# Expert 0's weight residuals: from VectorE to ScalarE and GpSimd, with the second search spaced wider

## The chip, the cores and the metric

One Trainium2 chip, one of its cores. The core has a matrix engine (TensorE, PE in the profile), VectorE (DVE), ScalarE (ACT), GpSimd (POOL) and an engine that mostly issues transfers (SyncE, SP). They run at the same time and wait for each other through semaphores. The metric is the device time of one execution in microseconds (us), the median over runs; lower is better.

## The reference, cut to what matters

Attention with two kinds of masks gives 4608 tokens of 512 numbers. A mixture of experts follows: experts and tokens are matched greedily, in order of the logit, until an expert has its 576 tokens; then each expert runs two matrix products with a relu between them.

```python
logits = x @ w_gate                       # x: attention output, [4608, 512]
order = np.argsort(-logits.flatten())
for idx in order:
    tok, e = int(idx) // E, int(idx) % E
    if assigned[tok] >= 0 or counts[e] >= cap:    # cap = 4608 // 8 = 576
        continue
    assigned[tok] = e
    counts[e] += 1
for e in range(E):
    mask = assigned == e
    h = np.maximum(x[mask] @ w1[e], 0.0)          # w1[e]: [512, 1024]
    out[mask] = h @ w2[e]                         # w2[e]: [1024, 512]
```

## The kernel before, in words

The first 205 us are attention and the logits. Then the experts are handled in the order in which they fill up (`ph` 0 to 7). For each of them the kernel finds which expert fills next, and at which logit, by a **search** over thresholds; loads that expert's weights; finds its tokens (`slots`, `indices`); gathers their rows (GpSimd's indirect transfers, tile xr); converts and transposes them (xg, xt); and runs the two layers (`ffn`). Expert 0's search comes alone, ahead of everything. The search for expert 1, its weights and its tokens run beside the matmuls of expert 0, those of expert 2 beside expert 1, and so on.

**Two halves of a weight.** [...] A float32 weight w, scaled by a power of two s, is split into an upper half hi = f16(w*s) and a lower half lo = f16(w*s - hi). `split` (L1011) does this in 8 pieces for w1 (128 columns of the 1024, for all four row blocks: 128 x 512 numbers, interleaved in memory) and 8 for w2 (one row block each, 128 x 512 too): ScalarE writes hi (L1013), VectorE lo (L1014). Before it `square` (L995, ScalarE, tile jk) and `scale` (L1001, a small matmul L1003, L202 to L207) find s. The tokens are split the same way; a product is hi\*hi + hi\*lo + lo\*hi. The float32 weights lie in one buffer for each of w1 and w2, so the next expert's loads wait for the last reader.

**Expert 0's matmuls.** `hidden` makes the first layer in chunks of 128 hidden units. For expert 0 eight chunks are made for rows 0 to 255 first, then eight for rows 256 to 575; each chunk is 12 matmuls, then a relu on ScalarE (hh, L1175) and the lower half on VectorE (hl, L1176). Chunk f needs piece f of w1h and w1l. The chunks' PSUM tiles (ph) cycle through three buffers; the transposes of token tile 2 take one of them between chunk 0 and chunk 1, so chunk 2 takes the buffer of chunk 0. The second layer (L1210, L1216) goes over token tiles 0, 4 (the tail of 64), 1, 2, 3; tile 0 takes the eight pieces of w2h and w2l in turn, 24 matmuls. ScalarE (and for the tail VectorE) takes each result out (y), and GpSimd scatters it to the output (L1227).

**What sets the order.** The kernel emits its instructions along a clock of its own: each matmul adds its nominal cost (109 units for 256 rows, 136 for 320, 123 for 288, 216 and 108 in the second layer), and side chains (`side`: search and slots; `fetch`: indices, gathers, conversions; `spread` and `slowly`: the pieces of weights) are advanced when their due time has passed. What a chain yields is the distance to its next step: in a search round `pace(T_COUNT)`, `pace(T_SUM)`, `pace(T_STEP)`, where `pace` multiplies by PACE1 in expert 1's search alone; T_HOT1 ahead of expert 1's index matmuls (L956), T_HOT for later experts. Each of the R1 = 7 rounds has a comparison on VectorE (cm, L812), nine count matmuls (L828), two small reductions (L831, L834), a folding matmul (L837), a threshold test (L844), a broadcasting matmul (L847) and the next candidates (L850). After the last, the next expert's number (ei) is known and its weights are loaded.

TensorE keeps emission order throughout (`MAN`); inside expert 0's `ffn` ScalarE does too (`MAN0`). The pieces of expert 0's w1 are all emitted ahead of `ffn`; its w2 pieces come from `second` at steps of 1000. VectorE's, GpSimd's and SyncE's orders, and ScalarE's from expert 1 on, are chosen by the compiler's scheduler by priority, before the run. An expert's `ffn` starts being emitted only when its `fetch` has been emitted to its end.

Of the kernel before, what the change touches and what calls it, by code (L numbers as in the profile page):

```python
# [12 lines left out]
AF = mybir.ActivationFunctionType  # L13
OP = mybir.AluOpType
# [33 lines left out]
SHI = CAP // SLO  # L48
URGENT = 4000
T_FIRST, T_COUNT, T_SUM, T_STEP, T_PREFIX, T_NEXT, T_HOT, T_DUP, T_LOAD = 1100, 2950, 1350, 1225, 3900, 2300, 4200, 550, 8000  # L50
PACE1 = 0.55
H0 = 256
HURRY = (0, 1, 7)
MAN, MAN0, MANP = {mybir.EngineType.PE}, {mybir.EngineType.Activation}, (0,)
# [2 lines left out]
T_ROWS, T_ROW = 5000, 1200  # L57
HEAT = (8, 18, 5)
SCALE_AT, TURN_AT, TAKE_AT, SEARCH_AT, TURN_U, W_EARLY, TURNS, TURN_E = 7, 9, 9, 10, 0, 1, 3, 2
T_F, T_LOAD0, T_HOT1, T_W, T_SQ, T_SCALE, T_CUT, T_BULK0 = 3000, 1500, 6350, 4000, 1500, 1500, 1500, 600  # L60
CUT0 = 1
EDGE0, PEAKS, PEAKS_N = 18, (24, 29), (1, 3)
LATE_Q, STORE_Q = (2, 3), (3, 4, 5)
V_BITS, W1_BITS, W2_BITS = 8, 7, 15
# [72 lines left out]
def band_stride_attention_then_capacity_moe(ctx, tc, qt, kl, ks, nl, ns, wg, w1, w2, cst, out, dbg=None):  # L137
    nc = tc.nc
# [593 lines left out]
    def urgent(ph=1):  # L732
        return tc.high_priority(offset=URGENT * (2 if ph == 0 else 1))

    def spread(ph, todo):
        for step, f in todo:
            if ph not in rush:
                yield step if ph else min(step, T_BULK0)
            f()
# [61 lines left out]
    def pace(t):  # L801
        return t if len(closed) > 1 else t * PACE1

# [167 lines left out]
    def weights(ph, ei):  # L971
        e = nc.sync.value_load(ei[0:1, 0:1], min_val=0, max_val=E - 1)
        res, todo = [], []
        for name, w, nch, width, bits in (("w1", w1, DC, FF, W1_BITS), ("w2", w2, FC, DM, W2_BITS)):
            wf = wp.tile([128, nch, width], F32, name=name)
# [6 lines left out]
            k = W_EARLY if ph == 0 and name == "w2" else 4  # L982
# [6 lines left out]
            sc = rt.tile([128, 2], I32, name="w_s" + name)  # L989
            hi = w16.tile([128, nch, width], F16, name=name + "h")  # L990
            lo = w16.tile([128, nch, width], F16, name=name + "l")
# [16 lines left out]
                    return [(slice(0, nch), slice(k, k + 128)) for k in range(0, width, 128)]  # L1008
                return [(slice(k, k + 1), slice(0, width)) for k in range(nch)]

            def split(c, f, k, wf=wf, sc=sc, hi=hi, lo=lo):  # L1011
                s_ = sc.bitcast(F32)[:, 0:1]
                nc.scalar.activation(hi[:, c, f], wf[:, c, f], AF.Copy, scale=s_)  # L1013
                nc.vector.scalar_tensor_tensor(lo[:, c, f], wf[:, c, f], s_, hi[:, c, f], op0=OP.mult,  # L1014
                                               op1=OP.subtract)

            todo.append([(T_SQ, lambda c=c, g=square: g(c)) for c in range(4)])
            todo.append([(T_SCALE, scale)])
# [3 lines left out]
        if ph == 0:  # L1022
# [7 lines left out]
            def more():  # L1030
                with urgent(0):
                    for _, f in cut1[:CUT0]:
                        f()
                g = spread(ph, cut1[CUT0:])
                chains.append([due_now(), g])
# [206 lines left out]
    def due_now():  # L1242
        return clock
# [10 lines left out]
    with tc.manual_schedule(engines=MAN):  # L1254
        work[0] = now[:4] + (now[4](),)
        chains.append([T_LOAD0, load0()])
        for ph in range(E):
            with tc.manual_schedule(engines=MAN0) if ph in MANP else nullcontext():
                while ph not in ready:
                    c = min(chains, key=lambda c: c[0])  # L1260
# [79 lines left out]
```

## Time and profile before

| | |
|---|---|
| median of 3 runs | 696.94 us (696.28 to 700.25) |
| the profiled execution | 691.74 us, its span 690.0 us |
| TensorE busy | 616.1 us, 89% of the span |
| VectorE, ScalarE, GpSimd busy | 460.6, 348.5, 110.5 us |
| expert 0's matmuls | from 238 to 301 us |
| mean granted TensorE clock | 0.939 |

The profile is one execution. Times in its rows are us from the start of the span. A timeline row gives start, duration, engine, line of the kernel, operation, output and inputs, shape, and how many instructions were merged; in brackets stands how long the engine stood idle before it, and what ended that. Busy time of PE is modelled, so the starts of matmuls tell more than their lengths. The granted clock is the share of TensorE's full clock that it was given.

### The profile page before, as it was taken

To read this page: it belongs to the slowest core of one execution; us is meant where nothing else is said; L and a number is where in the kernel's file an instruction comes from. 1 tells how busy PE (TensorE), PEld (TensorE's weight loads), DVE (VectorE), ACT (ScalarE), POOL (GpSimd) and SP (SyncE) were. 2 spreads that over 40 slices of the span, in tenths; PEclk is the share of its full clock that TensorE was granted. 3 is DMA by queue.
4 is the path that set the end of the run, shared out by engine and by line. 5 is a ranking of instruction groups with operands and counts; after the bars stand their busy time and mean duration, and the time that the engine had idled before them with its cause. 6 is when DMAs were issued, how large, how long until landed. Compare 5 with 4: busy or idle time off the path is not lost.

```text
span 690.0 us, 19782 instructions
## 1 busy us (share of the span) xinstructions
PE 616.1 (89%) x8294; PEld 406.7 (59%) x8298; DVE 460.6 (67%) x1389; ACT 348.5 (51%) x567; POOL 110.5 (16%) x124
## 2 busy tenths in 40 slices
PE   6989999899964788989989989999998998999993
PEld 3666777567744365458447537646646745645741
DVE  3757787677857879786787767778768657580200
ACT  2557656575420645681673565384286177771210
POOL 2101110011000300420240150041042041211011
PEclk9579999999975899999999999999999999999997
DMA  8958779777120720860870680491284188821010
GB/s 234 241 157 267 202 212 267 230 228 216 41 67 2 262 75 5 316 132 1 283 168 1 242 188 21 148 255 49 82 290 83 33 295 244 232 51 48 1 39 31
DMA packets 76364, 102.42 MB, mean 148 GB/s; under 512 B 41292, under 2 KB 49062, under 8 KB 75763
## 3 DMA queue, kind: packets, MB, share of 16 engines
q1 hardware_dynamic: 68195, 79.61, 40.4%
q0 software_dynamic: 7360, 21.15, 10.0%
q8 instruction: 65, 1.06, 0.7%
q10 hardware_dynamic: 720, 0.39, 0.2%
q14 instruction: 24, 0.20, 0.1%
HBM read 73.60 MB, written 18.87 MB: 134 GB/s over the span
## 4 chain that ended last, share of the span: by engine, by line
PE 20%; issue 14%; DVE 11%; DMA 10%; ACT 5%; POOL 4%; SPq 1%; POOLq 0%; DVEq 0%; ACTq 0%
PE ph L1168 15%; DMA w<-in_w_dram 6%; DMA xr<-x_scr,idx 3%; POOL xr L1073 2%; PE ph L1216 2%; DVE w1l L1014 2%; ACT jk L995 2%; DVE w2l L1014 2%; POOL out_dram L1227 1%; DVE hl L1176 1%; ACT hh L1175 1%; DMA xt<-xg 1%; DVE xg L1063 1%; DVE cm L812 1%; SPq L980 1%
## 5 line engine op out<-in xcount | busy, mean ns | idle before, releaser
L1168 PE MATMUL ph<-xt,w1h 128*128 128x288 f16 (+2 forms) x1024 | 177.1, 288 | 7.2 <-DMA xt<-xg 5.0
L1168 PEld LDWEIGHTS <-w1h 128*128 128x128 f16 x1024 | 97.3, 98 | 37.9 <-issue 7.7
L1168 PE MATMUL ph<-xt,w1l 128*128 128x288 f16 (+2 forms) x512 | 111.2, 288 | 0.0
L1227 POOL DMA_INDIRECT out_dram<-y,idx x40 | 48.9, 1222 | 332.4 <-ACT y L1226 304.7
L1216 PE MATMUL ph<-w2h,hh 128*128 128x512 f16 x256 | 97.7, 382 | 1.1 <-DVE hl L1176 1.1
L1175 ACT ACTIVATE hh<-ph 128x576 f16<-128x576 f32 (+2 forms) x72 | 42.7, 594 | 110.4 <-PE ph L1168 110.3
L995 ACT ACTIVATE jk<-w 128x1024 f16<-128x1024 f32 x64 | 67.4, 1054 | 60.3 <-DMA w<-in_w_dram 59.2
L1216 PE MATMUL ph<-w2h,hl 128*128 128x512 f16 x256 | 97.7, 382 | 0.0
L1216 PE MATMUL ph<-w2l,hh 128*128 128x512 f16 x256 | 97.5, 381 | 0.0
L1216 PEld LDWEIGHTS <-hh 128*128 128x128 f16 x512 | 49.4, 98 | 58.7 <-issue 8.8
L1176 DVE SCALAR_TENSOR_TENSOR hl<-ph,hh 128x576 f16<-128x576 f32 (+2 forms) x72 | 49.5, 687 | 46.0 <-ACT hh L1175 46.0
L1168 PEld LDWEIGHTS <-w1l 128*128 128x128 f16 x512 | 50.3, 98 | 14.0 <-issue 1.3
L1073 POOL DMA_INDIRECT xr<-x_scr,idx x40 | 41.8, 1046 | 51.7 <-DMA w<-in_w_dram 25.3
L372 ACT ACTIVATE pr<-spa 128x576 f32<-128x576 f32 x32 | 20.8, 651 | 55.9 <-PE spa L369 42.0
L1014 DVE SCALAR_TENSOR_TENSOR w1l<-w,w_sw,w1h 128x512 f16<-128x512 f32 x64 | 45.5, 745 | 4.8 <-ACT w1h L1013 4.8
L1014 DVE SCALAR_TENSOR_TENSOR w2l<-w,w_sw,w2h 128x512 f16<-128x512 f32 x64 | 46.3, 743 | 1.8 <-ACT w2h L1013 1.7
L1216 PEld LDWEIGHTS <-hl 128*128 128x128 f16 x256 | 25.1, 98 | 37.6 <-issue 12.6
L1226 ACT ACTIVATE y<-ph,so 128x512 f32<-128x512 f32 x32 | 21.8, 680 | 45.0 <-PE ph L1216 31.8
L1013 ACT ACTIVATE w1h<-w,w_sw 128x512 f16<-128x512 f32 x64 | 42.4, 708 | 3.0 <-DVE w_sw L207 1.8
L1013 ACT ACTIVATE w2h<-w,w_sw 128x512 f16<-128x512 f32 x64 | 41.2, 710 | 5.4 <-DVE w_sw L207 5.4
L423 POOL DMA_DIRECT2D x_scr<-xs x23 | 14.9, 656 | 170.5 <-DVE xs L407 123.2
L389 PE MATMUL po<-v_s,pr 64*54 64x65 f32 x768 | 33.4, 240 | 4.3 <-issue 4.3
(603 smaller groups left out, 967.1 us busy)
## 6 DMA issues: line engine op xcount, KB each, us to landing
w<-in_w_dram SPq DMA_DIRECT2D x64, 512.0 KB
kl<-in_kl_dram SPq DMA_DIRECT2D x16, 304.0 KB
v_s<-in_ns_dram SPq DMA_DIRECT2D x16, 292.5 KB
v_l<-in_nl_dram SPq DMA_DIRECT2D x16, 292.5 KB
ks<-in_ks_dram SPq DMA_DIRECT2D x16, 288.0 KB
qs<-in_qt_dram SPq DMA_DIRECT2D x16, 288.0 KB
ql<-in_qt_dram SPq DMA_DIRECT2D x16, 288.0 KB
x_scr<-xl SPq DMA_DIRECT2D x8, 512.0 KB
```

The source lines that it names most:

```text
L372: nc.scalar.activation(pr[:, :S].rearrange("k (h n) -> k h n", h=2), u.sp[p][:, :, :HS], AF.Exp, scale=0.125)
L389: nc.tensor.matmul(po[r:r + u.nq, j - j0], pr[k, o:o + u.nq], u.vn[k, t, 2 * p + h], start=(j == j0), stop=(j == j1 - 1), skip_group_check ...
L995: nc.scalar.activation(jk, wf[:, c * n4:(c + 1) * n4].rearrange("p c f -> p (c f)"), AF.Square, scale=1.41422, accum_out=sq[:, c:c + 1])
L1013: nc.scalar.activation(hi[:, c, f], wf[:, c, f], AF.Copy, scale=s_)
L1014: nc.vector.scalar_tensor_tensor(lo[:, c, f], wf[:, c, f], s_, hi[:, c, f], op0=OP.mult, op1=OP.subtract)
L1073: nc.gpsimd.indirect_dma_start(out=xr[:n], out_offset=None, in_=x_rows, in_offset=bass.IndirectOffsetOnAxis(ap=idx[:n, t:t + 1], axis=0))
L1168: nc.tensor.matmul(tile_[:, j, :w], wt[:, d, f * 128:(f + 1) * 128], xt[:, d // 2, xx, d % 2, c], start=(k == 0), stop=(k == 3 * DC - 1))
L1175: nc.scalar.activation(hv, src, AF.Relu)
L1176: nc.vector.scalar_tensor_tensor(lv, src, 0.0, hv, op0=OP.max, op1=OP.subtract)
L1216: nc.tensor.matmul(py, a[:, f, ts_], w[:, f], start=(k == 0), stop=(k == len(todo) - 1))
L1226: nc.scalar.activation(y, py, AF.Copy, scale=so[:, t:t + 1])
L1227: st = nc.gpsimd.indirect_dma_start(out=out_rows, out_offset=bass.IndirectOffsetOnAxis(ap=idx[:n, t:t + 1], axis=0), in_=y[:n], in_offset= ...
```

## The change

Three constants and `split` are edited. W_OWN says how many pieces of expert 0 keep VectorE's subtraction: two of w1, none of w2. For the other 14 ScalarE writes hi as before, then scales the float32 piece in place, and GpSimd subtracts hi from it. All pieces of experts 1 to 7 (`ph` true) stay as they were. PACE1 goes from 0.55 to 0.65, which spaces the steps of expert 1's search wider among expert 0's matmuls, and T_HOT1 from 6350 to 5000, which brings its index matmuls closer behind its slots.

```diff
-PACE1 = 0.55
+PACE1 = 0.65
...
-T_F, T_LOAD0, T_HOT1, T_W, T_SQ, T_SCALE, T_CUT, T_BULK0 = 3000, 1500, 6350, 4000, 1500, 1500, 1500, 600
+T_F, T_LOAD0, T_HOT1, T_W, T_SQ, T_SCALE, T_CUT, T_BULK0 = 3000, 1500, 5000, 4000, 1500, 1500, 1500, 600
 CUT0 = 1
+W_OWN = {"w1": 2, "w2": 0}
...
-            def split(c, f, k, wf=wf, sc=sc, hi=hi, lo=lo):
+            def split(c, f, k, wf=wf, sc=sc, hi=hi, lo=lo, own=W_OWN[name]):
                 s_ = sc.bitcast(F32)[:, 0:1]
                 nc.scalar.activation(hi[:, c, f], wf[:, c, f], AF.Copy, scale=s_)
-                nc.vector.scalar_tensor_tensor(lo[:, c, f], wf[:, c, f], s_, hi[:, c, f], op0=OP.mult,
-                                               op1=OP.subtract)
+                if ph or k < own:
+                    nc.vector.scalar_tensor_tensor(lo[:, c, f], wf[:, c, f], s_, hi[:, c, f], op0=OP.mult,
+                                                   op1=OP.subtract)
+                else:
+                    nc.scalar.activation(wf[:, c, f], wf[:, c, f], AF.Copy, scale=s_)
+                    nc.gpsimd.tensor_tensor(lo[:, c, f], wf[:, c, f], hi[:, c, f], op=OP.subtract)
```

## The prediction

> **What bounds the kernel now.** I read, in this order, the page's engine table, the timeline of each engine between 235 and 305 us, the waits of TensorE, and busy time by stretch.
>
> ```profile
> PE 616.1 (89%) x8294; PEld 406.7 (59%) x8298; DVE 460.6 (67%) x1389; ACT 348.5 (51%) x567; POOL 110.5 (16%) x124
> ...
> 241.30:244.00 2.70, 2.70 (x15) 2.20 (x15) 2.25 (x6) 1.28 (x3) 0.00 (x0) 0.50 0.83 273
> 244.00:256.30 12.30, 9.48 (x105) 8.12 (x104) 9.22 (x28) 4.90 (x11) 0.00 (x0) 0.99 0.22 49
> 256.30:273.50 17.20, 15.42 (x142) 10.69 (x140) 14.99 (x51) 10.82 (x22) 0.00 (x0) 1.00 0.00 1
> 273.50:301.20 27.70, 26.50 (x197) 12.79 (x195) 22.07 (x77) 19.44 (x34) 10.40 (x9) 1.00 0.88 260
> ```
>
> The columns of the four stretches are PE, PEld, DVE, ACT, POOL, then granted clock, DMA share and GB/s. TensorE carries the kernel. Expert 0 is these four stretches: both hidden passes (rows 0 to 255 of the expert, then the other 320), then its second layer. GpSimd is idle in both passes, VectorE is busy 9.2 of 12.3 and 15.0 of 17.2 us. TensorE's losses and the start of the next experts:
>
> ```profile
> 244.66 0.38 PE L1168 MATMUL ph<-xt,w1h 128*128 128x256 f16 x2
> 244.98 0.38 PE L1168 MATMUL ph<-xt,w1h 128*128 128x256 f16 x2
> ...
> 247.24 0.47 PE L828 MATMUL pr__4490<-ohn,cm 128*68 128x32 f16 x9 [1.44 <-DVE cm L812]
> 249.87 0.17 PE L837 MATMUL pr__4490<-r,fold 68*128 68x8 f16 x1 [1.38 <-DVE r L834]
> 252.43 0.45 PE L828 MATMUL pr__4558<-ohn,cm 128*68 128x32 f16 x9
> 256.70 0.43 PE L1168 MATMUL ph<-xt,w1h 128*128 128x320 f16 x2
> 271.47 0.17 PE L847 MATMUL pr__4812<-g,ones_j 128*128 128x8 f16 x1
> 273.53 0.38 PE L1216 MATMUL ph<-w2h,hh 128*128 128x512 f16 x1
> 275.47 0.23 PE L900 MATMUL pr__4929<-sc,tri 128*128 128x72 f16 x2
> 282.84 1.31 PE L956 MATMUL pr__5048<-ohl,rv 128*32 128x64 f16 x36
> 285.71 0.20 PE L964 MATMUL pr__5090<-pick,p 128*64 128x10 f16 x2 [0.81 <-DVE p L959]
> 303.41 0.54 PE L1168 MATMUL ph<-xt,w1h 128*128 128x288 f16 x3 [1.91 <-DMA xt<-xg]
> ...
> 357.96 0.78 PE L1168 MATMUL ph<-xt,w1h 128*128 128x288 f16 x4
> 358.82 0.65 PE L1168 MATMUL ph<-xt,w1h 128*128 128x288 f16 x4
> ```
>
> In the hidden passes TensorE, which runs a fixed order, stands for the search's matmuls behind VectorE (1.44, 1.38). At expert 1 it stands 1.91 us for the transposed tokens (xt), not for weights. At expert 2 four matmuls take 0.78 instead of 0.65: xt arrives just in time there, with no slack. So what moves the end is **when xt of expert 1 and of expert 2 lands**; both chains begin at the index matmuls (L956), whose place among expert 0's matmuls is set by the constants that the change edits.
>
> **The change part by part.** First, the 14 subtractions. Removed from VectorE, put on ScalarE and GpSimd:
>
> ```profile
> L1014 DVE SCALAR_TENSOR_TENSOR w1l<-w,w_sw,w1h x64: 730/746/798, 236.7 to 610.3; 128x512 f16<-128x512 f32 x64
> ...
> 236.74 1.41 DVE L1014 SCALAR_TENSOR_TENSOR w1l<-w,w_sw,w1h 128x512 f16<-128x512 f32 x2
> ...
> 237.82 3.78 ACT L1013 ACTIVATE w1h<-w,w_sw 128x512 f16<-128x512 f32 x6
> 241.95 0.38 ACT L1175 ACTIVATE hh<-ph 128x256 f16<-128x256 f32 x1 [0.35 <-PE ph L1168]
> 265.27 0.44 ACT L1175 ACTIVATE hh<-ph 128x320 f16<-128x320 f32 x1 [1.42 <-PE ph L1168]
> ...
> 247.24 0.42 DVE L1176 SCALAR_TENSOR_TENSOR hl<-ph,hh 128x256 f16<-128x256 f32 x1
> ...
> L246 POOL MEMSET v_s<- 128x1560 f32 x2 | 2.8, 1388 | 0.0
> ```
>
> VectorE loses 14 x 0.75 = 10.4 us. ScalarE gains 14 operations at 3.78 / 6 = 0.63, 8.8 us. A GpSimd subtraction is not in this trace. From below: 0.75, VectorE's price for the shape. From above: the memset writes 1560 numbers in 1.39 us, 0.46 for 512; two reads and a write at that rate are 1.4. I take 1.3, nearer the row of the same engine; both ends stay in the range. [...]
>
> *First pass.* The split of pieces is emitted before the first relu, and ScalarE keeps emission order there (row 237.82 stands before 241.95). Twelve operations now stand where six were: 237.82 + 12 x 0.63 = 245.4. The first relu moves from 241.95 to 245.4, ends at 245.8, its hl (0.42) at 246.2. The third chunk of hidden units takes the PSUM buffer of the first, so it starts at 246.2, not 244.66. Pieces are ready: the last subtraction ends near 246.8 and its chunk comes last. From 246.2 come six chunks of 12 matmuls at 0.11 (the spacing of rows 244.66 and 244.98, three matmuls apart) = 7.9, and two search rounds at about 0.35 each without waits (the count's 0.45 overlaps the next matmul), as VectorE is now free: 254.8, against 256.70. **Gain 1.9.**
>
> *Second pass.* 96 matmuls of 0.109 x 320/256 = 0.136 are 13.1; the wider search leaves three rounds in it (1.1) instead of four; the matmul of w2's scale waits 0.5, because ScalarE is late with its squares; 0.8 for search waits that remain. 254.8 + 15.5 = 270.3, against 273.53. ScalarE needs 1.26 us a piece plus a relu of 0.44 per 1.65 us of matmuls, so its relus lag up to about 2 us; three PSUM buffers hide this (0 as long as the lag is below two chunks, 3.3 us). GpSimd's last piece comes near 272.5, and the second layer needs it 21 matmuls of 0.216 after its start (274.8): hidden, and 2 us of cover. Together **expert 0's second layer starts 3.2 us earlier.**
>
> *Search positions.* A round costs 0.55 x (2950 + 1350 + 1225) + 100 = 3139 units of emission clock (about a ns of matmul), after it 0.65 x 5525 + 100 = 3691. Followed yield by yield (each step comes with the first matmul past its due time), L956 of expert 1 moves from 8.64 to 11.66 thousand units behind the start of the second layer; T_HOT1 has taken 1.35 of it back. The old position agrees with the trace: 282.84 - 273.53 = 9.3 us. New: 270.3 + 11.66 + 0.7 = 282.7. Its operands on VectorE took until 281.9 (row below), 6.4 us behind L900; L900 will be at 277.0, so they may come as late as 283.4. I take 282.9, 0.1 later than before. So the gain of expert 0 is spent on the search's new place.
>
> ```profile
> 280.88 1.02 DVE L948 TENSOR_TENSOR ohl<-sh,iota 128x768 f16<-128x768 f16 x2
> 284.20 0.74 DVE L1224 SCALAR_TENSOR_TENSOR y<-ph,so,yl 64x512 f32<-64x512 f32 x1 [2.29 <-ACT yl L1223]
> ...
> 286.44 0.98 POOL L1073 DMA_INDIRECT xr<-x_scr,idx  x1 [0.30 <-DVE idx L968]
> 292.24 1.40 POOL L1073 DMA_INDIRECT xr<-x_scr,idx  x1 [0.30 <-issue]
> ...
> DMA to landing us min/median/max: 3.4/3.8/5.6
> ...
> 295.87 0.69 ACT L1226 ACTIVATE y<-ph,so 128x512 f32<-128x512 f32 x1 [0.57 <-PE ph L1216]
> 296.98 1.05 ACT L995 ACTIVATE jk<-w 128x1024 f16<-128x1024 f32 x1
> 298.01 0.62 ACT L1062 ACTIVATE xg<-xr 64x512 f16<-64x512 f32 x1
> ```
>
> *What is late next.* L964 waited 0.81 because VectorE first did the tail's y (284.20); that y now comes 3 us earlier, so the gathers start near 285.7, not 286.44. The fifth lands 5.8 + 3.8 later, 295.3. Its conversion stood at 298.01 behind a y that waits for TensorE (295.87) and a square (296.98); that y comes 3 us earlier too, so I put the conversion at 295.8: **expert 1 starts 2.2 us earlier, at 301.2**. TensorE has no work from 270.3 + 26.9 = 297.2 on (27.7 for the layer, less the 0.8 of L964), so it idles 4 us instead of 2.
>
> *The clock.* Long waits cost more than their length:
>
> ```profile
> 575.10 0.28 PE L1168 MATMUL ph<-xt,w1h 128*128 128x288 f16 x1 [0.63 <-DMA xt<-xg]
> 577.89 0.54 PE L1168 MATMUL ph<-xt,w1h 128*128 128x288 f16 x3 [2.52 <-DMA xt<-xg]
> ...
> 578.70:582.00 3.30, 3.30 (x16) 2.05 (x15) 3.03 (x5) 2.04 (x4) 0.00 (x0) 0.50 1.00 353
> 302.00:304.00 2.00, 0.59 (x5) 0.49 (x6) 1.56 (x8) 0.92 (x3) 1.15 (x1) 1.00 0.35 54
> 304.00:306.00 2.00, 2.00 (x21) 1.62 (x20) 1.33 (x2) 1.72 (x3) 0.00 (x0) 1.00 0.34 131
> ```
>
> After a wait of 2.5 us (3.2 with the one before it) the granted clock was 0.50 for 3.3 us, a loss of 1.6; after 1.91 us at expert 1 it stayed at 1.00. Four us lie beyond both: **+1.6**, bounds 0 and 1.7. [...]
>
> *Expert 2.* Its L956 stood 13.8 thousand units ahead of the end of expert 1's matmuls, and will stand 11.9 ahead; from expert 3 on the distance is as before (14.0, 13.8). With no slack (row 357.96) its xt is 1.9 us late; I take **+1.8**; bounds 0 (a faster chain, as at expert 1) and 3.5 (with a halved clock).
>
> *Sum:* -2.2 + 1.6 + 1.8 = +1.2 us. The profiled execution took 691.74 (span 690.0 and 1.74 around it), 0.75% below the median of 696.94 (696.28 to 700.25). Its difference carried over gives 698.1.
>
> **The rivals.** *Taking turns (slower).* VectorE's two-operand instructions on the search's loop (the new candidate, and cm, 0.79) may have to stand aside while GpSimd reads two operands, up to 1.3 each. No row shows GpSimd and VectorE reading together. A round has 3.69 + 0.36 = 4.05 us on TensorE, the free loop takes 3.4 (count at 252.43, next cm done at 255.79, row below), so 0.65 is free, and a round can lose 2 x 1.3 - 0.65 = 1.95.
>
> ```profile
> 254.99 0.80 DVE L812 TENSOR_TENSOR cm<-rmn,cand 128x612 f16<-128x612 f32 x1
> ```
>
> At 1.7 for each of the three rounds beside w2's subtractions expert 0's second layer starts at 275.4, L956 and all behind it 5.1 later: +6.3, **703.2**. It decides from 0.8 us a round on. For it: TensorE's order leaves no way round. Against: between two subtractions GpSimd waits for ScalarE. [...]
>
> *The gain is kept (faster).* The conversions of expert 1 follow their gathers without any hold: 285.7 + 5.8 + 3.8 + 0.62 + about 3.7 from conversion to first matmul (as 298.01 + 0.62 to 303.41 is 4.8, less 1.1 of queueing) = 299.6, -3.8; the wait is then 2.4 us, the clock stays, and expert 2's chain closes up as well, to 0. **693.1.** For it: ScalarE's holds of before. Against: the token conversions of expert 1 are emitted later, the last four behind the y of 295.87.
>
> *The subtractions don't leave ScalarE free.* If writing a piece in place had to wait until GpSimd has read the piece before (they interleave in memory), a piece would cost 0.63 + 1.3, the first relu would come near 250, all 4.6 later: **702.7**. Against: ScalarE wrote piece 3 at 237.82 while VectorE still read piece 2 of the same tile (236.74 + 1.41 = 238.15).
>
> **How the numbers follow.** Forecast 0.50, own range 694.5 to 700.4; taking turns 0.21; in-place wait 0.04; gain kept 0.25. From 0.5% on (3.5 us) a measurement of this kernel can tell a difference. Nearly all of the forecast lies within it; the slow rivals are slower, the fast one faster by a little more than that: faster 0.24, same 0.50, slower 0.26. The range takes the fast rival (692.5) and the slow ones (703.5) in.
>
> **What would show it.** Right: the first relu of expert 0 on ScalarE near 245.4, expert 0's second layer from about 270, L956 within 1 us of 282.84, expert 1 from about 301 after a wait of 3 to 5 us with clock 0.50 behind it, a new wait for xt at expert 2. Wrong: search matmuls waiting over 0.8 us each in the second pass, subtractions far from 1.3 us, expert 2 starting without a wait, or experts 3 to 7 shifting against each other.

## The result, and the profile after

The changed kernel took 704.6 us (median of 19 executions) beside 696.94 us for the kernel before (19 executions); the ratio is 1.0129, 95% interval 1.0097 to 1.0161. (Ratios and intervals leave out the executions that were slowed as a whole, medians don't, so a ratio is not the quotient of the two medians.) It is **slower by 1.3%**, some 8 to 9 us. The forecast was 698.1 with a range from 692.5 to 703.5, so it missed. The profiled execution took 701.34 us (span 699.6), the one before 691.74 (span 690.0).

To read where the 9.6 us between the two profiles arise, three matmuls of the kernel before are needed: the first of expert 0, the first of expert 1's second layer, and the first of expert 3.

```profile
237.97 0.27 PE L1168 MATMUL ph<-xt,w1h 128*128 128x256 f16 x1 [1.03 <-ACT xt L1055]
...
328.28 0.38 PE L1216 MATMUL ph<-w2h,hh 128*128 128x512 f16 x1
...
413.99 0.65 PE L1168 MATMUL ph<-xt,w1h 128*128 128x288 f16 x4
```

The same places and the waits of TensorE in the changed kernel, from its timeline (lines lie 1 to 5 further down: L1173 is the first layer, L1221 the second, L957 the index matmuls, L965 what follows them, L1004 the matmul of a weight's scale):

```profile
238.91 0.27 PE L1173 MATMUL ph<-xt,w1h 128*128 128x256 f16 x1 [0.74 <-ACT xt L1060]
...
243.34 0.27 PE L1173 MATMUL ph<-xt,w1l 128*128 128x256 f16 x1
247.92 0.38 PE L1173 MATMUL ph<-xt,w1h 128*128 128x256 f16 x2 [4.31 <-ACT xt L1060]
...
273.10 0.39 PE L1221 MATMUL ph<-w2h,hh 128*128 128x512 f16 x1
...
280.57 0.24 PE L901 MATMUL pr__4973<-sc,tri 128*128 128x72 f16 x2
...
286.36 1.29 PE L957 MATMUL pr__5060<-ohl,rv 128*32 128x64 f16 x36
...
288.33 0.20 PE L965 MATMUL pr__5102<-pick,p 128*64 128x10 f16 x2
...
304.68 0.16 PE L1004 MATMUL pr__5299<-ss,ones_b 128*128 128x1 bf16 x1 [2.31 <-DVE ss L1002]
304.78 0.28 PE L1173 MATMUL ph<-xt,w1h 128*128 128x288 f16 x1
307.50 0.42 PE L1173 MATMUL ph<-xt,w1h 128*128 128x288 f16 x1 [2.44 <-DMA xt<-xg]
...
335.15 0.38 PE L1221 MATMUL ph<-w2h,hh 128*128 128x512 f16 x1
...
366.59 0.54 PE L1173 MATMUL ph<-xt,w1h 128*128 128x288 f16 x3 [0.36 <-DMA xt<-xg]
...
422.70 0.65 PE L1173 MATMUL ph<-xt,w1h 128*128 128x288 f16 x4
```

The busy time of its engines over the whole span, from the page:

```profile
PE 617.5 (88%) x8294; PEld 405.3 (58%) x8298; DVE 453.6 (65%) x1375; ACT 357.4 (51%) x581; POOL 127.3 (18%) x138
```

And its busy time by stretch (PE, PEld, DVE, ACT, POOL; then granted clock, DMA share, GB/s):

```profile
247.92:252.00 4.08, 4.08 (x29) 3.19 (x30) 3.03 (x5) 1.57 (x4) 4.08 (x5) 0.58 0.26 51
252.00:273.10 21.10, 20.77 (x198) 15.85 (x196) 15.49 (x54) 17.10 (x33) 10.01 (x8) 1.00 0.06 10
273.10:304.78 31.68, 27.70 (x205) 13.17 (x205) 22.79 (x79) 21.18 (x38) 15.51 (x13) 1.00 0.78 231
307.50:313.00 5.50, 5.50 (x25) 3.52 (x26) 3.55 (x11) 2.56 (x4) 0.00 (x0) 0.50 0.01 3
```

The work moved as it should: VectorE has 7 us less, ScalarE 9 and GpSimd 17 us more. TensorE's own work is the same (8294 matmuls); it lost time waiting and at half clock. From expert 0's first matmul to expert 3's first ("the stretch" from here on), 176.02 us became 183.79, and this holds 7.8 of the 9.6 us:

| part of the stretch | before | after | difference | forecast |
|---|---|---|---|---|
| first matmul to expert 1's tokens (303.41; 307.50) | 65.44 | 68.59 | +3.15 | -2.2 |
| on to expert 1's second layer (328.28; 335.15) | 24.87 | 27.65 | +2.78 | +1.6 |
| on to expert 3's first matmul (413.99; 422.70) | 85.71 | 87.55 | +1.84 | +1.8 |

The other 1.8 us lie ahead of expert 0 (0.94) and behind expert 3's first matmul (0.89), where nothing was edited. Single executions differ by more than that: expert 0's first matmul comes between 234.4 and 245.0 us in the traces of this case.

**How much of it is clock.** Summed in steps of 0.5 us, the time that the granted clock took from the stretch (1 minus the clock, times the step) is 3.4 us before and 5.1 after. The kernel before has half clock there too: once beside expert 0's first two chunks, once in expert 2's second layer. So between these two traces 1.7 of the 7.8 us are clock and some 6 are waits. Over the executions behind the ratios, each with its mean granted clock, an estimate is that time x clock grew by 3.9 us (656.8 to 660.7) and time x (1 - clock) by 4.1 (39.3 to 43.4), each give or take 2: on average about half of the loss is clock.

**The first layer of expert 0** took 34.19 us instead of 35.56. Its gain is small because TensorE stood 4.31 us ahead of the third chunk, then ran 4.08 us at 0.58 of its clock. ScalarE's timeline, and a row of VectorE's, show what it stood for:

```profile
238.74 0.72 ACT L1014 ACTIVATE w1h<-w,w_sw 128x512 f16<-128x512 f32 x1
239.50 0.72 ACT L1019 ACTIVATE w<-w,w_sw 128x512 f32<-128x512 f32 x1
240.12 0.71 ACT L1014 ACTIVATE w1h<-w,w_sw 128x512 f16<-128x512 f32 x1
...
246.95 0.36 ACT L1180 ACTIVATE hh<-ph 128x256 f16<-128x256 f32 x1
247.22 0.59 ACT L1060 ACTIVATE xt<-ph 128x512 f16<-128x512 f32 x1
...
247.35 0.42 DVE L1181 SCALAR_TENSOR_TENSOR hl<-ph,hh 128x256 f16<-128x256 f32 x1 [2.69 <-ACT hh L1180]
```

Twelve operations take 8.21 us (0.68 each), and only then comes the first relu, 8.04 us after the first matmul instead of 3.98. The third chunk's buffer waits for the relu and its lower half. The profile names the copy xt behind the relu, which ends at 247.81; the lower half ends at 247.77, 0.15 us ahead of the chunk at 247.92. In a later run (e13) the lower half ends at 249.42 and the chunk again comes 0.15 behind it, at 249.57, though xt had ended at 249.27; so it is most likely the lower half. All of them stand behind the twelve operations.

**Behind expert 0's second layer** the index matmuls come 13.26 us after the layer's start (9.31 before), and expert 1's matmuls run on, with the last of its tokens, 4.1 us later than before on the trace's clock. TensorE is out of work by then: it waits 2.31 us for the scale of expert 1's w2 and 2.44 for the tokens, and then runs 5.5 us at half clock.

### The profile page after: what moved, and what is told of

It reads as the page before. It is cut to its first block, busy times and chain, and to the rows that moved or that the text cites. A ratio compares the mean times of both kernels' runs of the same rounds, so it can differ in the third digit from the quotient of the medians.

```text
span 699.6 us, 19801 instructions
## 1 busy us (share of the span) xinstructions
PE 617.5 (88%) x8294; PEld 405.3 (58%) x8298; DVE 453.6 (65%) x1375; ACT 357.4 (51%) x581; POOL 127.3 (18%) x138
## 4 chain that ended last, share of the span: by engine, by line
PE 48%; issue 15%; DVE 13%; DMA 10%; ACT 8%; POOL 4%; SPq 1%; POOLq 0%; ACTq 0%; DVEq 0%
PE ph L1173 17%; PE po L390 6%; PE ph L1221 5%; PE spa L347 4%; DMA w<-in_w_dram 3%; DMA xr<-x_scr,idx 3%; DMA xt<-xg 3%; POOL xr L1078 2%; PE spb L441 2%; PE spb L502 2%; PE spa L370 1%; DVE w1l L1016 1%; ACT w L1019 1%; PE spb L461 1%; POOL out_dram L1232 1%
## 5 line engine op out<-in xcount | busy, mean ns | idle before, releaser
L1173 PE MATMUL ph<-xt,w1h 128*128 128x288 f16 (+2 forms) x1024 | 178.9, 291 | 12.5 <-DMA xt<-xg 5.6
L1173 PEld LDWEIGHTS <-w1h 128*128 128x128 f16 x1024 | 98.5, 99 | 43.4 <-DMA xt<-xg 6.2
L1173 PE MATMUL ph<-xt,w1l 128*128 128x288 f16 (+2 forms) x512 | 112.4, 291 | 0.0
L1221 PE MATMUL ph<-w2h,hh 128*128 128x512 f16 x256 | 97.1, 379 | 0.3 <-DVE hl L1181 0.3
L1221 PE MATMUL ph<-w2h,hl 128*128 128x512 f16 x256 | 97.0, 379 | 0.0
L1221 PE MATMUL ph<-w2l,hh 128*128 128x512 f16 x256 | 97.0, 379 | 0.0
L1221 PEld LDWEIGHTS <-hh 128*128 128x128 f16 x512 | 48.6, 98 | 63.2 <-issue 12.8
L1173 PEld LDWEIGHTS <-w1l 128*128 128x128 f16 x512 | 50.5, 99 | 14.5 <-issue 1.5
L1078 POOL DMA_INDIRECT xr<-x_scr,idx x40 | 41.3, 1031 | 56.8 <-DVE L L922 25.2
L1221 PEld LDWEIGHTS <-hl 128*128 128x128 f16 x256 | 25.0, 97 | 34.7 <-issue 9.2
L1016 DVE SCALAR_TENSOR_TENSOR w1l<-w,w_sw,w1h 128x512 f16<-128x512 f32 x58 | 41.0, 743 | 5.0 <-ACT w1h L1014 5.0
L1016 DVE SCALAR_TENSOR_TENSOR w2l<-w,w_sw,w2h 128x512 f16<-128x512 f32 x56 | 40.5, 742 | 1.6 <-ACT w2h L1014 1.4
L1068 DVE TENSOR_TENSOR xg<-xr,xg 128x512 f16<-128x512 f32 (+1 forms) x37 | 25.9, 705 | 17.3 <-ACT xg L1067 17.2
```

The source lines that it names most:

```text
L1068: nc.vector.tensor_tensor(xs[:, 1], xv, xs[:, 0], op=OP.subtract)
L1078: nc.gpsimd.indirect_dma_start(out=xr[:n], out_offset=None, in_=x_rows, in_offset=bass.IndirectOffsetOnAxis(ap=idx[:n, t:t + 1], axis=0))
L1173: nc.tensor.matmul(tile_[:, j, :w], wt[:, d, f * 128:(f + 1) * 128], xt[:, d // 2, xx, d % 2, c], start=(k == 0), stop=(k == 3 * DC - 1))
L1221: nc.tensor.matmul(py, a[:, f, ts_], w[:, f], start=(k == 0), stop=(k == len(todo) - 1))
```

## The experiments

The theory after the result: **two losses**. (1) Six doubled pieces of w1 hold the first relu on ScalarE; TensorE idles and is slowed. (2) The wider spacing takes the search's waits out of expert 0's first layer, but places the index chains of experts 1 and 2 so late that the time is lost again, with a half clock on top. Rivals: the GpSimd subtractions themselves cost (late start, or VectorE standing aside); the late squares of w2 cost; the lost time is expert 2's.

All runs are against the kernel before on the same chip. "Run on" is when expert 1's matmuls run on after the last wait for tokens; all us are counted from expert 0's first matmul and come from one execution each, the ratio from many.

| run | pieces on GpSimd | constants | first relu | first layer | run on | stretch | ratio (95%) |
|---|---|---|---|---|---|---|---|
| before | 0 | old | 3.98 | 35.56 | 65.44 | 176.0 | 1 |
| e1 | 14 | old | 8.04 | 35.86 | 65.75 | 176.8 | 0.9995 (0.9958 to 1.0033) |
| e4 | w2's 8 | old | 4.55 | 36.03 | 66.44 | 176.8 | 1.0004 (0.9964 to 1.0044) |
| e2 | 0 | new | 3.52 | 30.92 | 64.20 | 179.5 | 1.0068 (1.0031 to 1.0106) |
| e5 | w2's 8 | new | 4.16 | 31.65 | 65.24 | 181.1 | 1.0045 (1.0007 to 1.0084) |
| e9 | 3 + 8 | new | 5.79 | 32.66 | 66.57 | 180.0 | 1.0123 (1.0053 to 1.0193) |
| **after** | 14 | new | 8.04 | 34.19 | 68.59 | 183.8 | 1.0129 (1.0097 to 1.0161) |
| e8 | 14 | PACE1 old | 8.04 | 36.24 | 66.78 | 177.8 | 1.0030 (0.9989 to 1.0070) |
| e11 | 14 | new, places back | 8.05 | 34.20 | 65.89 | 177.6 | 1.0038 (0.9993 to 1.0083) |
| e7 | 0 | new, places back | 3.51 | 30.79 | 62.91 | 174.9 | 0.9982 (0.9945 to 1.0020) |

### The two halves of the change alone

e1_split_only: the 14 subtractions with the old constants.

```diff
-PACE1 = 0.65
+PACE1 = 0.55
...
-... T_HOT1, ... = 3000, 1500, 5000
+... T_HOT1, ... = 3000, 1500, 6350
```

> The 14 subtractions on GpSimd, the old constants (PACE1 0.55, T_HOT1 6350). Theory A (the loss comes from the search's new place: TensorE reaches expert 1's index matmuls 3 thousand units later, and the chains of experts 1 and 2 with them): expert 0's first layer starts its second part about as in the changed kernel (34 to 35 us after its start), the wait at expert 1 is that of before or less, and the time is the kernel before's, -2 to +2 us. Theory B (the loss comes from the split: ScalarE's in-place scaling holds the first relu, TensorE idles 4.3 us and its clock is halved behind it): +5 to +9 us.

e2_const_only: the constants with every subtraction on VectorE.

```diff
-W_OWN = {"w1": 2, "w2": 0}
+W_OWN = {"w1": 8, "w2": 8}
```

> The new constants alone (PACE1 0.65, T_HOT1 5000), all 16 subtractions on VectorE. Theory A: slower by 4 to 9 us: a wait of 2 us or more for w2's scale and another for xt at expert 1, clock 0.50 behind it, and 1 to 3 us at expert 2. Theory B: -2 to +2 us, since the first layer is as before and its search waits are shorter.

e4_w2_only: the old constants, and only w2's eight pieces on GpSimd.

```diff
+PACE1 = 0.55 and T_HOT1 = 6350, as in e1
-W_OWN = {"w1": 2, "w2": 0}
+W_OWN = {"w1": 8, "w2": 0}
```

> Only the eight pieces of w2 on GpSimd, all of w1 on VectorE, old constants. The first relu is not held, so there is no idle time of 4 us in the first pass and no halved clock behind it. Theory A: 0 to 3 us faster than the kernel before, as three rounds of the search no longer share VectorE with w2. Theory B: the same as A here, but 5 us or more faster than the kernel with all 14 pieces and the old constants; under A the difference between the two is under 3 us.

Measured: 697.37, 702.04 and 695.99 us beside 698.66. The subtractions alone change nothing that could be told, all of them or w2's; the constants alone cost 0.7%; both together cost 1.3%, where the sum of the two is 0.6, give or take 0.5. In e1 the relu is held just as long (8.04 us), and TensorE waits as well:

```profile
251.19 0.59 PE L1173 MATMUL ph<-xt,w1h 128*128 128x256 f16 x2 [2.49 <-ACT xt L1060]
```

But from this third chunk on (9.01 us after the first matmul, 6.69 before) the layer needs 26.85 us instead of 28.87, since VectorE answers the search sooner: no search matmul waits over 0.3 us there. The hold and this gain cancel. In e2 the first layer is the shortest of these, 4.6 us under before, and the second layer with the wait at its end takes 4.8 us more than the 27.7 before; busy time in the two layers, and behind it the wait at the end of the second, from the timeline:

```profile
239.49:270.41 30.92, 27.24 (x263) 21.05 (x263) 27.88 (x84) 20.11 (x40) 0.00 (x0) 1.00 0.21 63
270.41:302.94 32.53, 27.73 (x206) 13.08 (x204) 23.47 (x80) 19.35 (x34) 11.63 (x10) 1.00 0.79 230
```

```profile
302.84 0.16 PE L1004 MATMUL pr__5285<-ss,ones_b 128*128 128x1 bf16 x1 [3.23 <-DVE ss L1002]
```

So each half alone takes away the same thing, TensorE's waits for VectorE in the search (1.44 and 1.38 before; 0.57 and 0.82 in e2, none in e1). Behind the third chunk the changed kernel takes 25.18 us, e1 26.85: where the spacing has taken most of the waits away, the subtractions have little left to win, and their hold is nearly a plain loss.

### The held relu

e5_new_w2 puts w1's six pieces back on VectorE; e9_three_pieces puts three of them back. Both keep the new constants.

```diff
-W_OWN = {"w1": 2, "w2": 0}
+W_OWN = {"w1": 8, "w2": 0}     # e5
+W_OWN = {"w1": 5, "w2": 0}     # e9
```

> The changed kernel with the six w1 pieces back on VectorE: only the eight w2 pieces are subtracted by GpSimd, with both new constants. The stretch from expert 0's first matmul to expert 3's first (short: the stretch to expert 3) took 176.0 us before, 179.5 with the constants alone and 183.8 in the changed kernel. Theory A (the w1 pieces hold the first relu on ScalarE, TensorE stands 4.3 us for it and runs at half clock afterwards; w2's pieces cost nothing, as with the old constants): expert 0's first layer falls from 34.2 to about 31 us, the stretch to about 179.5, the time to that of the constants alone, 0.6 to 0.8% above before. Rival B (any subtraction on GpSimd costs once the search is spaced wider, for instance through VectorE's loop): first layer over 33, time 1.0 to 1.3% above before.

> The changed kernel with three of w1's six pieces back on VectorE (pieces 5 to 7 and all of w2 stay on GpSimd), both new constants. Theory A (what costs is that ScalarE does two operations a piece ahead of the first relu, at 0.74 us the second): the first relu comes 3 x 0.74 = 2.2 us earlier against expert 0's first matmul, TensorE's wait before the third chunk falls from 4.3 to 1.5 to 2.6 us, expert 0's first layer from 34.2 to 32 to 33.3, time 0.5 to 1.0% above before (between the 0.45% with no w1 piece and the 1.29% with six). Rival B (not the number of pieces, but that GpSimd is used in the first pass at all): wait over 3.5 us, first layer over 33.8, time as the changed kernel.

e5 came out at 1.0045 (0.6 to 0.8% was expected), its first layer at 31.65 us, so w1's six pieces cost the changed kernel about 0.8%, give or take 0.5. Its stretch of 181.1 is over the 179.5 expected. In e9 the first relu comes 5.79 us after the first matmul, 2.25 us sooner, and the wait is 2.38:

```profile
248.11 0.36 ACT L1180 ACTIVATE hh<-ph 128x256 f16<-128x256 f32 x1
...
249.07 0.38 PE L1173 MATMUL ph<-xt,w1h 128*128 128x256 f16 x2 [2.38 <-ACT xt L1060]
```

Relu, wait and layer (32.66) follow the number of doubled pieces as expected. The ratio, 1.0123, is above the expected 1.005 to 1.010, with an interval too wide (1.0053 to 1.0193) to tell half of the loss from all of it.

### GpSimd's late first subtraction

In the changed kernel GpSimd did nothing for 8.46 us ahead of its first subtraction, although the first scaled piece was there at 240.2. The instructions of that line, with durations as min/median/max in ns, and the timeline:

```profile
L1020 POOL TENSOR_TENSOR w1l<-w,w1h x6: 1143/1146/1602, 246.8 to 253.3; 128x512 f16<-128x512 f32 x6
L1020 POOLq MODIFY_POOL_CONFIG  x2: 42/42/43, 238.3 to 238.4; - x2
```

```profile
246.81 7.62 POOL L1020 TENSOR_TENSOR w1l<-w,w1h 128x512 f16<-128x512 f32 x6 [8.46 <-ACT w1h L1014]
```

Two configuration instructions of 0.04 us stand at its start. The trace has no busy time of GpSimd's in the 8.46 us, 6.6 of them behind the first scaled piece, and what fills them is not shown. e3_early_gpsimd and e10_early_clean put a tiny subtraction behind the all-reduce at 206 us, to see whether the gap then falls earlier.

```diff
     nc.gpsimd.partition_all_reduce(rng, pk, 128, bass.bass_isa.ReduceOp.max)
+    early = r1.tile([128, 1], F32, name="early")
+    nc.gpsimd.tensor_tensor(early, rng, pk, op=OP.subtract)    # e3
+    nc.gpsimd.tensor_tensor(early, pk, pk, op=OP.subtract)     # e10
```

> The changed kernel, with one more GpSimd subtraction of a single column right after its reduction over partitions at 206 us, so that its first subtraction of weights is not the first of its kind. In the changed kernel GpSimd stood idle for 8.46 us between 238.35 and 246.81 although the first scaled piece lay ready at 240.2. If that was a change of GpSimd's program, the first subtraction now starts at 240 to 241. Theory C (the late subtractions hold TensorE in the first pass): 3 to 5 us faster than the changed kernel. Theories A and B: no faster than it by more than 1 us, for TensorE's third chunk (247.92) waits for the first relu and its hl (end 247.77) as well.

> The changed kernel with one tiny two-operand GpSimd operation put behind the all-reduce, this time on data that nobody waits to write again, so that GpSimd's 8.5 us before its first subtraction fall where it has nothing to do. Theory A (the late start of GpSimd does not set the pace, ScalarE's two operations a piece do): subtractions from within 2.5 us of the first scaled piece, TensorE's wait before the third chunk still 4.0 to 4.6 us, first layer 34 to 35, time within 0.4% of the changed kernel. Rival B (the late subtractions hold the chunks of the first pass): wait under 3 us, first layer under 33, time 0.4% or more below the changed kernel.

e3 took 714.06 us (1.0242, 1.0194 to 1.0289), but it measured another thing: its tiny operation reads rng, which VectorE then overwrites, and VectorE stood 7 us for that gap, just ahead of the first search.

```profile
212.32 0.15 DVE L709 TENSOR_SCALAR rng<-rng 128x1 int32<-128x1 int32 x1 [6.99 <-POOL early L708]
```

e10 avoids that. GpSimd's first subtraction now starts at once, and the relu comes exactly when it did, 8.05 us after the first matmul at 243.88:

```profile
245.27 1.16 POOL L1022 TENSOR_TENSOR w1l<-w,w1h 128x512 f16<-128x512 f32 x1 [3.85 <-ACT w L1021]
...
251.93 0.36 ACT L1182 ACTIVATE hh<-ph 128x256 f16<-128x256 f32 x1
```

The ratio is 1.0147 (1.0082 to 1.0212), no better than the changed kernel: ScalarE's order sets the pace, not GpSimd. The wait ahead of the third chunk was 2.72 and the layer 32.95, both outside the theory's numbers and inside the rival's. The third chunk started 9.03 us after the first matmul, as in the changed kernel (9.01); the first two chunks took 6.31 us of that (9.03 less 2.72) beside 4.70 there, and the rest of the layer 23.92 beside 25.18. By these times an estimate is that in this execution the half clock fell on the first two chunks, which filled part of the wait, and not behind it.

### The late squares of w2

e6_squares_early brings expert 1's weight preparation forward, so that the scale of w2 is no longer late.

```diff
+        if ph == 1:
+            todo = [(min(s, T_W if i == 0 else 1000), f) for i, (s, f) in enumerate(todo)]
```

> The changed kernel with one edit: for expert 1 the steps of its weight preparation stand 1000 units apart instead of 1500, so that the last squares of w2 are emitted before the end of expert 0's matmuls and not behind them. Theory A (the 2.31 us wait for the scale of w2 covers the wait for the transposed tokens that follows it; the tokens land no sooner): the wait for the scale falls under 0.5 us, the wait for the tokens grows from 2.4 to 4 to 5 us, expert 1's hidden matmuls run on from within 0.7 us of where they did, time within 0.3% of the changed kernel. Rival B (the late squares are the cost): expert 1 about 2.3 us earlier, time 0.3 to 0.6% below the changed kernel.

The wait for the scale of w2 is gone, and the wait for tokens is twice as long; the half clock stays (timeline of TensorE, then the stretch behind it with its clock of 0.52).

```profile
311.25 0.28 PE L1175 MATMUL ph<-xt,w1h 128*128 128x288 f16 x1 [2.50 <-DMA xt<-xg]
314.05 0.42 PE L1175 MATMUL ph<-xt,w1h 128*128 128x288 f16 x1 [2.52 <-DMA xt<-xg]
```

```profile
314.05:319.50 5.45, 5.45 (x26) 3.50 (x27) 3.91 (x9) 2.00 (x4) 0.00 (x0) 0.52 0.01 3
```

Expert 1 runs on after 69.08 us, 0.5 later than in the changed kernel; the ratio is 1.0116 (1.0069 to 1.0163), not told apart from it. The edit moved the squares of expert 1's w1 as well, and its token indices came 0.6 us later against expert 0's first matmul, so the test is not clean. But expert 1 followed its tokens, and the 2.31 us of the changed kernel only covered a wait for them.

### The place of the index chains

e8_pace_back undoes PACE1 alone in the changed kernel. e7_places_back keeps the new constants with all subtractions on VectorE and sets three places back; e11_changed_places does this in the changed kernel.

```diff
-PACE1 = 0.65
+PACE1 = 0.55                                   # e8
...
-        yield T_PREFIX
+        yield 2000 if ph == 1 else T_PREFIX    # e7, e11: with e6's edit, and
-... (T_F if 1 < ph < E - 1 else 0) ...
+... (1000 if ph == 2 else T_F if 1 < ph < E - 1 else 0) ...
```

> The changed kernel with one constant undone: the search's spacing 0.55 again, T_HOT1 stays 5000, all 14 pieces on GpSimd. Theory A (the wider spacing is what moves the index chains of experts 1 and 2 and what leaves TensorE without work while the first relu is held): stretch to expert 3 of 175 to 177.5 us, as with the split alone (176.8), time within 0.4% of before. Rival B (the index matmuls brought nearer to the prefix matmul by T_HOT1 now wait for VectorE, and are the loss): a wait of 0.5 us or more at the index matmuls of expert 1, time 0.5% or more above before.

> The constants alone (all pieces on VectorE), with expert 1's weight steps 1000 units apart, the prefix matmul of expert 1 due 2000 instead of 3900 units after its number, and expert 2's index chain due 1000 instead of 3000 units after its prefix matmul. Theory A (the wider spacing shortens expert 0's first layer by 4 to 5 us; all of it is lost again because the index chains of experts 1 and 2 and expert 1's squares are late against the matmuls): the stretch to expert 3 falls from 179.5 to 173 to 176 us, the time to 0 to 0.6% below before. Rival B (the loss of the constants is not in these places, but in waits that follow from elsewhere, such as the gathers or ScalarE's load): stretch 178 to 180, time still 0.5% or more above before.

> The changed kernel, 14 pieces on GpSimd, with the three places set back (expert 1's weight steps 1000 units apart, its prefix matmul due 2000 instead of 3900 units after its number, expert 2's index chain due after 1000 instead of 3000). Theory A (two separate losses: the late index chains and the held relu): the places give back what they gave back to the constants alone, about 0.9%, the held relu stays: first layer 34 to 35, stretch to expert 3 from 183.8 to 177 to 180, time 0.2 to 0.7% above before. Rival B (they are one loss: with the relu held the places do not matter, or the other way round): time over 1.0% above before, or first layer under 32.

With the old spacing (e8) the loss falls from 1.29% to 0.30%, which can't be told from none; the stretch of 177.8 is just over the 177.5 expected. The rival's wait is there too, as T_HOT1 = 5000 brings the index matmuls ahead of what they read, but it does not decide:

```profile
284.68 1.50 PE L957 MATMUL pr__5031<-ohl,rv 128*32 128x64 f16 x36 [1.07 <-DVE rv L943]
```

With the places back, the constants alone go from 1.0068 to 0.9982 and the whole change from 1.0129 to 1.0038: 0.9% both times (give or take 0.5), as the theory has it. In e11 the first layer stays at 34.20 (the held relu), and expert 1 runs on 2.7 us sooner than in the changed kernel, at full clock:

```profile
307.10:313.00 5.90, 3.85 (x32) 2.96 (x33) 5.44 (x17) 4.89 (x9) 1.09 (x1) 1.00 0.40 95
```

In the stretch the two losses are separate and nearly add up: against the changed kernel, places back (e11) takes off 6.2 us, w1 back on VectorE (e5) 2.7, and both (e16, below) 8.3. In the whole time only the loss of the places is clear; e16 doesn't come out below e11. e7 (696.15 us beside 697.71) beats the changed kernel, but cannot be told from the kernel before.

### Which place, and a better version

e12_places_rows is e7 with the token conversions of expert 1 due 800 instead of 1200 units apart. e13_expert1_back and e14_expert2_back set back expert 1's and expert 2's places one at a time in the changed kernel; e15_constants_expert1 sets back expert 1's with the constants alone; e16_w2_places is e11 with w1 on VectorE.

```diff
-            yield T_ROWS if t == 0 else T_ROW
+            yield T_ROWS if t == 0 else 800 if ph == 1 else T_ROW    # e12
```

> The constants alone with the three places set back, as the run that came out at 0.9982, and with the token conversions of expert 1 due 800 instead of 1200 units apart, so that the last two are emitted ahead of a square. Theory A (expert 1's first matmuls still wait 0.75 and 2.25 us for tokens whose conversion stands behind other work on ScalarE): that wait falls by 1 to 1.5 us, time 0.3 to 0.6% below before. Rival B (the transposing transfers and the weight loads set the landing): wait unchanged within 0.5 us, time 0 to 0.3% below before.

> The changed kernel with expert 1's places set back alone (its weight steps 1000 units apart, its prefix matmul due after 2000 instead of 3900 units). All three places together took 1.0129 to 1.0038 of before. Theory A (expert 1's chain is most of the loss, expert 2's about 1.8 us as predicted): expert 1's hidden matmuls run on within 66.5 us of expert 0's first matmul (68.6 in the changed kernel) with no half clock behind, expert 2 still waits; ratio to before 1.004 to 1.008. Rival B (expert 2's chain is most of it): ratio 1.009 or more.

> The changed kernel with expert 2's index chain alone set back (due after 1000 instead of 3000 units). Theory A: expert 1 as in the changed kernel (hidden matmuls run on 68 to 69 us after expert 0's first, clock 0.50 behind), the time from there to expert 3's first matmul 1 to 2.5 us shorter than the changed kernel's 115.2; ratio to before 1.009 to 1.012. Rival B: ratio 1.007 or less.

> The constants alone, with expert 1's places set back and expert 2's left late. If setting expert 2's chain back is what lengthens the stretch behind expert 3 (267 to 269 us in the three runs that had it, 264 to 266.7 in nearly all others), this run has 264 to 266.5 there, a stretch to expert 3 of 175.5 to 177.5, and a ratio to before of 0.997 to 1.001. If that is scatter between executions, the stretch behind may come out anywhere from 264 to 269, and the ratio is 0.999 to 1.004.

> The changed kernel with w1 on VectorE, only w2's eight pieces on GpSimd, and all three places set back. Theory A (both losses of the change taken away, w2's pieces cost nothing): first layer of expert 0 under 31.8 us, stretch to expert 3 of 174 to 177, ratio to before 0.996 to 1.001. Rival B (w2's pieces cost something once the places are back): stretch over 177.5, ratio over 1.002.

| run | first layer | run on | stretch | behind the stretch | ratio (95%) |
|---|---|---|---|---|---|
| e12 | 30.78 | 62.79 | 175.9 | 267.3 | 1.0035 (0.9990 to 1.0079) |
| e13 | 34.95 | 66.58 | 182.5 | 266.0 | 1.0084 (1.0046 to 1.0121) |
| e14 | 34.98 | 69.84 | 186.3 | 268.8 | 1.0129 (1.0056 to 1.0202) |
| e15 | 30.79 | 62.56 | 176.3 | 269.4 | 1.0025 (0.9987 to 1.0063) |
| e16 | 30.00 | 61.91 | 175.5 | 271.9 | 1.0055 (1.0022 to 1.0088) |

Expert 1's places alone give back 0.45% (e13), and 0.43% with the constants alone (e15), each give or take 0.5: in e13 expert 1 runs on 2.0 us sooner than in the changed kernel, after 66.58, but the clock behind that is 0.69 for 5.5 us, where the theory had no loss. Expert 2's place alone (e14) gives nothing, against the expectation; with expert 1's the two give 0.9% (e11), but the intervals are too wide to say that expert 2's has a share. In e12 the wait for the tokens of expert 1 fell as expected, from 2.25 to 1.10 us, and the time did not: 1.0035, over both theories' numbers, though not told apart from e7's 0.9982. e16 has both losses taken away, shows it in the first layer and the stretch, and is still 0.55% slower than before, a miss. (A cost of w2's pieces does not explain this: e12 and e15, which have none on GpSimd, show the same behind the stretch.)

What e16 loses against the kernel before, and e12 and e15 within their intervals, lies behind the stretch, which itself is as short as before (175.5 to 176.3; 176.0 before): from expert 3's first matmul to the last they take 267.3 to 271.9 us, where the kernel before took 264.3 and the changed one 265.2. e7 and e11 have it too (268.8 and 269.1), and e7 has the lowest ratio of all, so this is not a fixed price. e15 has it without expert 2's edit, so that edit alone is not the cause. The traces show where it arises. The granted clock costs 3.4 to 5.1 us there in these five runs, 1.7 before and in the changed kernel. In e15 and e16 TensorE also waits longer for VectorE in the second layers of experts 3 and 4, mostly for the sums of the searches that run there: 8.6 and 7.5 us in all, 4.6 before. Over all executions e16's time x clock is 657.1 us beside the 656.8 of the kernel before, its time x (1 - clock) 42.0 beside 39.3: by this estimate most of what it loses is clock. **Why the clock and these waits get worse there stays open.**

## Why the prediction was wrong, point by point

**Right in direction.** The held relu, the index chain that spends the gain of the first layer, a halved clock behind expert 1's wait, and 1.8 us up to expert 3 were all forecast; so was a GpSimd subtraction of 1.3 us (1.15 measured). **The step that failed is the term for expert 1's start:** it was put 2.2 us earlier than before and came 3.2 later, counted from expert 0's first matmul. Four sizes in it were too kind (the first layer by 1.9 us, the distance to the index matmuls by 0.7, the step to the gathers by 0.9, the gathers to the tokens by 1.95), the clock term behind it was too small by 1.2, and all errors go the same way.

**The first layer: a gain of 3.2 forecast, 1.4 measured.** The third chunk was put 8.2 us after the first matmul; it came after 9.0, since a doubled piece takes ScalarE 1.37 us and not 1.26. The rest was put at 24.1 us and took 25.2: the prediction had TensorE wait for the chunk (the search no longer filled the time), but charged no clock for it. The stretch behind it ran at 0.58, which costs 4.08 x 0.42 = 1.7 us; without that the 24.1 would have been 0.6 too long. At expert 1 the prediction had put a half clock behind a long wait, from the 0.50 for 3.3 us that the trace of the kernel before shows behind 2.52 us.

**L956: forecast 282.9, measured at 286.36 (now L957).** 2.8 us of that is the later start of the second layer (273.10, not 270.3; 0.9 of it from ahead of expert 0), 0.7 the distance.

**From the index matmuls to the gathers: 2.8 forecast, 3.69 measured, 3.60 before.** L965 lost its wait, as predicted, but another took its place. VectorE's indices stood behind the sum of expert 1's w1 squares, which waits for ScalarE:

```profile
289.55 0.16 DVE L1002 TENSOR_REDUCE ss<-sq 128x1 bf16<-128x4 f32 x1 [1.61 <-ACT jk L996]
289.62 0.16 DVE L968 CAST idx<-pr__5102 128x10 int32<-128x10 f32 x1
...
290.05 0.99 POOL L1078 DMA_INDIRECT xr<-x_scr,idx  x1 [2.82 <-DVE idx L969]
```

**From the first gather to expert 1: 15.5 forecast, 17.45 measured, 16.97 before.** The prediction let ScalarE's holds of the last conversion go; the chain did not get shorter. These three steps and the first layer make expert 1's start a loss of 3.2 us, where 2.2 were to be gained.

**The clock at expert 1: +1.6 forecast, +2.8 measured.** TensorE had not waited 4 us but 2.31 and 2.44 with two short matmuls between, and the half clock behind that lasted 5.5 us and not 3.3.

**Expert 2: +1.8 forecast, +1.84 measured**, but hardly for the reason given. The new wait for its tokens was 0.36 us. In expert 2's second layer TensorE waited 4.5 us in all, mostly for VectorE's share of the next search, where it had waited 2.1 before; but before, that layer had lost 1.7 us to the clock, and now none. The longest such waits, before and after:

```profile
404.61 0.17 PE L837 MATMUL pr__6690<-r,fold 68*128 68x8 f16 x1 [2.13 <-DVE r L834]
...
413.91 0.17 PE L838 MATMUL pr__6703<-r,fold 68*128 68x8 f16 x1 [2.55 <-DVE r L835]
```

And e14, with expert 2's chain set back, was no faster. That the figure came out is luck: it is the rest of other terms, and the mechanism is not shown.

**Taking turns** got a chance of 0.21 and was not the cause, though the time came out near its number. VectorE's instructions do get longer beside GpSimd's subtractions: the token residual took 1.20 instead of 0.69, one candidate step 0.65 instead of 0.24, and one step that adds a column to a table (pre, L821) 1.2 instead of 0.23 (the row holds two instructions). A comparison that started just ahead of a subtraction, at 267.17, kept its 0.80, and there the subtraction took 1.77 instead of 1.15 (the first of the three in GpSimd's row).

```profile
251.10 1.20 DVE L1068 TENSOR_TENSOR xg<-xr,xg 64x512 f16<-64x512 f32 x1
...
253.82 0.65 DVE L851 SCALAR_TENSOR_TENSOR cand<-steps,pr__4511,pre 128x18 f32<-128x18 f32 x1 [0.32 <-PE pr__4511 L848]
264.07 1.35 DVE L821 TENSOR_SCALAR pre<-steps,cand 128x18 f32<-128x18 f32 x2
267.17 0.80 DVE L813 TENSOR_TENSOR cm<-rmn,cand 128x612 f16<-128x612 f32 x1
...
267.20 4.16 POOL L1020 TENSOR_TENSOR w2l<-w,w2h 128x512 f16<-128x512 f32 x3 [0.58 <-POOL w2l L1020]
```

No search matmul of TensorE waited over 0.3 us in the second pass, and e4 prices w2's subtractions at nothing that could be told (1.0004, 0.9964 to 1.0044). Where the two ran together the trace has 0.4 to 1.0 us more in VectorE's instruction (1.20, 0.65 and 1.2 us) or 0.6 more in GpSimd's (1.77); which of the two pays is not shown. **Gain kept** fell with the gather chain, and the **in-place wait** did not show: ScalarE went on from piece to piece, 1.37 us apart, while GpSimd had not begun.

## What to carry to other kernels

Two edits that take away the same wait can't add their gains, while their costs both stay: run each alone before they are priced together. A step put on an engine that keeps an order is paid by whatever stands behind it there (here the first relu, 8.04 us after the first matmul instead of 3.98). And TensorE paid again in its clock behind some of its waits (1.7 us behind the 4.31 in the changed kernel, nothing behind the 1.91 at expert 1 in the kernel before), so such a wait needs a second price, with bounds.

## What the runs showed of the hardware

In the traces of the kernel before and of the changed one the half clock came in pieces that cost 1.7 us each or a whole multiple of it, ahead of expert 0, in the stretch and behind it. From expert 0's first matmul to the last one they are, in the kernel before, 3.41 us at 0.50 from 240.7, 404.6 and 578.6 us on, and in the changed one 3.41 us from 248.5 and 589.8 and 6.83 us from 306.5, the first 1.0 of them in the wait. The loss was not in proportion to the wait ahead of it: the same wait of 4.14 us ahead of the third chunk goes with a loss of 1.7 us in e11 (clock 0.95 over the 34.20 us of the first layer), and in e14 with matmuls at half clock for over 4 us (245.96 to 250.33), which costs over 2 us. Nor did the wait alone tell whether half clock followed: ahead of expert 1, waits of 0.74 and 2.19 us (e16) were followed by it, for about 3.5 us, while waits of 0.75 and 2.25 (e7) or of 0.88 and 2.05 (e11) were not. What decides it is not shown.

GpSimd stood idle for 6.9 us ahead of the early subtraction in e10 and for 8.46 us ahead of the first piece of w1 in the changed kernel, each the first two-operand instruction after the all-reduce. The later ones show no such gap: 0.2 to 0.6 us in the changed kernel, but for one that waited for ScalarE. ScalarE's pair of a conversion and an in-place scale of the same 128x512 piece came 1.37 us apart, 0.11 more than two conversions of 0.63; the trace does not show why.
